# A three-stage kernel on one core: its last stage regrouped into steps of two or three score units

## The chip, the cores and the metric

The kernel runs on one core of a Trainium2 chip. A core has five engines that run side by side, each through its own list of instructions in order: TensorE (PE: matmuls and transposes; PEld is its weight load), VectorE (DVE), ScalarE (ACT), GpSimd (POOL) and SyncE (SP, which here issues nearly all DMAs). They wait for one another through semaphores. Matmul results land in PSUM, eight banks of 128 x 512 fp32; the rest lies in SBUF. The metric is the time of one execution on the device in microseconds (us).

## The reference, cut to what matters

Three layers for 8 batch entries of 576 tokens: a pooled attention, a gated MLP with a spatial mix (together the first stage of the kernel), and, in the second stage, a mixture of four attention experts:

```python
logits = x @ w_gate                       # (576, 4); the two best experts, softmax over them -> w
for e in range(4):
    q, k, v = x @ wq[e], x @ wk[e], x @ wv[e]           # (576, 64) each
    scores = scale * (q @ k.T); scores[causal] = -1e9
    a = exp(scores - max); a /= a.sum(-1) + 1e-09
    out += (1 if e chosen else 0) * w_e * (a @ v @ wo[e])
```

fp32 accuracy is kept by splitting operands into a high and a low part (names that end in h and l): most products are two or three matmuls.

## The kernel before, in words

The first stage (class PhaseA) ends at about 595 us and is not touched. The second stage (class PhaseB) takes one batch entry b after the other, and in each two pairs of experts, p = 0 and 1: sixteen half batches. The work of a half batch is

- `proj` (tile pj): q and k of the pair, each in two halves of 288 tokens, 12 matmuls a half; `put_q` and `put_k` split the result on ACT and DVE and send copies of it by DMA (kd, qz) that the scores read;
- nine score units u = 0 to 8 (table `QT`): a block of 128 tokens of one expert. u = 0 is the last 64 tokens of both experts (576 columns, two banks, tile s4 in the code), u = 1 to 4 are blocks of 512, 384, 256 and 128 columns of the first expert, u = 5 to 8 the same of the second;
- each unit is `score` (PE; then a DVE reduction on L831, or L822 and L824 for u = 0, that adds the mask and gives the minimum of the negated scores; then exp on ACT, L834, which also gives the row sum), `scale` (DVE adds 1e-9, L845 or L843, and takes the reciprocal, L846; POOL, or DVE where the sets `SDF` and `SDL` say so, multiplies the row by reciprocal and gate weight, L850), and `trans` (PE transposes of 128 x 128, L863 and L876; ACT copies the high part, DVE subtracts the low part: tiles pbh, pbl);
- `av` (tile av, L896): attention times values for one expert, in two column parts, from pbh and pbl; then tiles ah and al (L906, L907);
- once both pairs are done, `outp` (tile op, L918 to L920): four output columns f, each in two column parts of 6 matmuls, copied by ACT (L921) and sent out.

Values and gate of the next entry (`vproj`, tile vp, five token tiles; `gate`, a chain of small DVE instructions that ends in tiles gw and wl) are computed in the second half batch of the one before. Everything in PSUM takes the next of eight banks in turn (`bank`), so a PE instruction waits until the bank that was given out eight earlier has been read.

The order is written by hand in `run`, one unit per step: score of unit k, `scale` of unit k - 1, then the fillers that the tables `FILL`, `FIRSTF` (first entry) and `LASTF` (last entry) name for this place (10 to 13: the four proj halves of pair 1; 00 to 03: those of the next entry's pair 0; v0 to v4 and g: values and gate; o: outp; x: loads), then av where it is due, and the transposes of unit k - 3 (`LAG`). `PRE` is what runs ahead of the first score. Within that order each engine's own list is merged by the scheduling layer.

Of the kernel before, what the change touches and what calls it, by code (L numbers as in the profile page):

```python
# [8 lines left out]
F32 = mybir.dt.float32  # L9
# [589 lines left out]
LAG = 3  # L599
# [9 lines left out]
PRE = 'v0 00 01 02 03 v1 v2 v3 v4 g'  # L609
# [3 lines left out]
class PhaseB:  # L613


    def __init__(self, ctx, tc, w, ins, x2d, out, ident):
# [3 lines left out]
        self.X, self.QK, self.V, self.GW, self.U, self.PT, self.AV, self.AH = {}, {}, {}, {}, {}, {}, {}, {}  # L620
# [185 lines left out]
    def score(self, b, p, u):  # L806
# [4 lines left out]
        st = w.tile([128, 8], F32, name="sm", bufs=4)  # L811
        pt = self.pr[:, (18 * b + 9 * p + u) % 5]
        if e == 2:
            parts = []
            for s in (slice(0, 320), slice(320, S)):
# [6 lines left out]
            nc.vector.tensor_tensor_reduce(o, o, self.ml, -0.125, BIG, OP.add, OP.min, st[:, 4:5])  # L822
            o = parts[0][0]
            nc.vector.tensor_tensor_reduce(o, o, self.mk[:, 0:1].to_broadcast([128, 320]), -0.125, st[:, 4:5],  # L824
                                           OP.add, OP.min, st[:, 0:1])
        else:
# [4 lines left out]
            nc.vector.tensor_tensor_reduce(o, o, self.mk[:, 576 - n:576], -0.125, BIG, OP.add, OP.min, st[:, 0:1])  # L831
            parts = [(o, slice(0, n))]
        for j, (o, s) in enumerate(parts):
            nc.scalar.activation(pt[:, s], o, AF.Exp, bias=st[:, 0:1], scale=-1.0, accum_out=st[:, 1 + 4 * j:2 + 4 * j])  # L834
        self.U[b, p, u] = (pt, st)

    def scale(self, b, p, u):
        nc = self.nc
        i, e = QT[u]
        pt, st = self.U[b, p, u]  # L840
        gw, wl = self.GW[b]
        if e == 2:
            nc.vector.tensor_scalar(st[:, 2:3], st[:, 1:2], 1e-9, st[:, 5:6], op0=OP.add, op1=OP.add)  # L843
        else:
            nc.vector.tensor_scalar(st[:, 2:3], st[:, 1:2], 1e-9, None, op0=OP.add)  # L845
        nc.vector.reciprocal(st[:, 3:4], st[:, 2:3])  # L846
# [3 lines left out]
         nc.gpsimd).tensor_scalar(pt[:, :n], pt[:, :n], st[:, 3:4], g, op0=OP.mult, op1=OP.mult)  # L850

    def trans(self, b, p, u):
        nc, w = self.nc, self.w
        i, e = QT[u]
        pt, _ = self.U.pop((b, p, u))
# [53 lines left out]
    def outp(self, b, f):  # L909
        nc, w = self.nc, self.w  # L910
        c = slice(128 * f, 128 * f + 128)
        o = w.tile([128, S], F32, tag="vg", name="o", bufs=3)
        for lo, up in AVS:
            ps = self.bank("op")[:, :up - lo]
            s = slice(lo, up)
            for p in range(2):
                ah, al = self.AH[b, p]
                nc.tensor.matmul(ps, self.wo[0][:, p, c], ah[:, s], start=p == 0, stop=False)  # L918
                nc.tensor.matmul(ps, self.wo[1][:, p, c], ah[:, s], start=False, stop=False)
                nc.tensor.matmul(ps, self.wo[0][:, p, c], al[:, s], start=False, stop=p == 1)  # L920
            nc.scalar.activation(o[:, s], ps, AF.Copy)  # L921
        nc.sync.dma_start(self.out[b, :, f], o)

    def run(self):
# [6 lines left out]
        units = [(b, p, u) for b in range(B) for p in range(2) for u in range(9)]  # L931
        def item(b, x):
# [4 lines left out]
            if x[0] == "1":  # L937
                return [part(b, 1)[int(x[1])]]
            if b + 1 == B:
                return []  # L940
# [5 lines left out]
        for x in PRE.split():  # L946
            for f in item(0 if x[0] == "1" else -1, x):
                f()
        for k in range(len(units) + LAG + 1):
            if k < len(units):  # L950
# [55 lines left out]
```

## Time and profile before

| | us |
|---|---|
| median of 3 runs (lowest, highest) | 986.61 (985.52, 988.78) |
| the profiled execution: its time | 986.47 |
| its span | 984.4 |
| the second stage in it, from its first matmul to the end | about 388 |

| engine | PE | PEld | DVE | ACT | POOL |
|---|---|---|---|---|---|
| busy us of the span | 915.4 | 863.3 | 715.2 | 511.1 | 490.4 |

The shares are averages over stages. In the second stage PE, DVE and ACT are all far busier than POOL. Matmuls overlap in the pipeline: how long one takes of PE's time is read from start to start of neighbours, not from its duration; the same holds, to a smaller degree, for DVE and ACT.

### The profile page before, as it was taken

Reading aid. Unit: us, or ns where it says so; the run is one execution under the profiler, and the core shown is the slowest. Engines: PE = TensorE matmul, PEld = TensorE weight load, DVE = VectorE, ACT = ScalarE, POOL = GpSimd, SP = SyncE. Lnnn points to the kernel's source line nnn. Section 1 sums busy time; section 2 is a strip of 40 time slices with the busy share of each in tenths; the row PEclk is TensorE's granted clock in tenths of the full one; section 3 lists DMA queues with packets and bytes.
Section 4 is the critical chain, followed back from the end, with each engine's and each line's share of the span. In section 5 each row is a group of like instructions: output and inputs, shape, how many; then the busy total and the mean of one; then the engine's idle time right before and its main releaser. Section 6 shows DMA issues by size and latency. Waiting matters only on the chain.

```text
span 984.4 us, 18357 instructions
## 1 busy us (share of the span) xinstructions
PE 915.4 (93%) x6488; PEld 863.3 (88%) x6488; DVE 715.2 (73%) x1901; ACT 511.1 (52%) x1291; POOL 490.4 (50%) x670
## 2 busy tenths in 40 slices
PE   4577899999999999999999999799999999999997
PEld 3366889989989999899899899799999999899987
DVE  6998747757567567476577524998979797979785
ACT  5576334334243343242342433576767676767776
POOL 6863727648369367375584450234434242525221
PEclk9589899999999999999999999999999999999999
DMA  9430321302302304122024012324233323322121
GB/s 331 186 101 22 101 88 47 128 26 81 110 20 71 118 12 141 45 82 99 31 62 121 1 52 70 84 48 118 72 112 72 116 74 96 84 84 84 48 60 73
DMA packets 37819, 82.92 MB, mean 84 GB/s; under 512 B 4960, under 2 KB 11104, under 8 KB 36832
## 3 DMA queue, kind: packets, MB, share of 16 engines
q1 hardware_dynamic: 37584, 81.75, 26.5%
q8 instruction: 52, 0.85, 0.4%
q14 instruction: 39, 0.32, 0.1%
q10 hardware_dynamic: 144, 0.00, 0.0%
HBM read 49.23 MB, written 18.87 MB: 69 GB/s over the span
## 4 chain that ended last, share of the span: by engine, by line
PE 57%; DVE 25%; ACT 8%; POOL 5%; issue 4%; DMA 1%; SPq 0%; POOLq 0%; ACTq 0%; DVEq 0%
PE op L445 4%; PE op L446 3%; PE op L447 3%; PE sp L420 3%; PE sp L422 3%; PE sp L421 3%; PE sc L230 3%; PE av L896 3%; DVE vnl L390 2%; DVE vnh L392 2%; ACT pr L834 2%; PE t L876 2%; PE tr L281 2%; DVE bs L376 2%; PE pj L705 2%
## 5 line engine op out<-in xcount | busy, mean ns | idle before, releaser
L850 POOL TENSOR_SCALAR pr<-pr,sm,gw 128x128 f32<-128x128 f32 (+3 forms) x119 | 77.9, 655 | 157.6 <-DVE sm L846 127.1
L834 ACT ACTIVATE pr<-s,sm 128x256 f32<-128x256 f32 (+4 forms) x160 | 83.0, 520 | 42.0 <-DVE sm L845 17.1
L332 POOL TENSOR_TENSOR xu<-x 128x576 f32<-128x576 f32 x28 | 39.2, 1428 | 98.3 <-DVE x L327 85.4
L446 PE MATMUL op<-g,woh 128*128 128x288 f32 x256 | 76.6, 301 | 4.2 <-POOL g L433 3.8
L420 PE MATMUL sp<-wsh,vnh 128*128 128x288 f32 x256 | 78.4, 306 | 1.6 <-ACT vnh L388 1.6
L404 PE MATMUL up<-x,wih 128*128 128x288 f32 x256 | 76.9, 301 | 2.4 <-ACT vg L364 2.2
L445 PE MATMUL op<-g,woh 128*128 128x288 f32 x256 | 78.2, 308 | 0.0
L421 PE MATMUL sp<-wsh,vnl 128*128 128x288 f32 x256 | 76.1, 297 | 0.0
L422 PE MATMUL sp<-wsl,vnh 128*128 128x288 f32 x256 | 75.9, 297 | 0.0
L406 PE MATMUL up<-x,wil 128*128 128x288 f32 x256 | 75.7, 296 | 0.0
L705 PE MATMUL pj<-xbh,wql 128*128 128x288 f32 x256 | 75.5, 295 | 0.0
L704 PE MATMUL pj<-xbl,wqh 128*128 128x288 f32 x256 | 75.5, 295 | 0.0
L703 PE MATMUL pj<-xbh,wqh 128*128 128x288 f32 x256 | 75.5, 295 | 0.0
L405 PE MATMUL up<-x,wih 128*128 128x288 f32 x256 | 75.1, 293 | 0.0
L447 PE MATMUL op<-g,wol 128*128 128x288 f32 x256 | 75.0, 297 | 0.0
L282 ACT ACTIVATE pth<-tr 128x640 fp32r<-128x640 f32 (+1 forms) x40 | 26.2, 654 | 79.6 <-PE tr L281 70.0
L876 PE MATMUL t<-ident,pr 128*128 128x128 f32 x320 | 57.9, 280 | 9.4 <-POOL pr L850 6.0
L831 DVE CUSTOM_DVE_ANT_0 s<-s,mk 128x512 f32<-128x512 f32 (+3 forms) x128 | 62.5, 488 | 0.4
L881 DVE TENSOR_TENSOR pbl<-t,pbh 128x512 fp32r<-128x512 f32 (+3 forms) x128 | 60.7, 484 | 2.4 <-ACT pbh L880 1.4
L230 PE MATMUL sc<-kbd,qt 128*128 128x144 f32 (+1 forms) x320 | 50.3, 303 | 10.9 <-DMA qt<-q_in 8.5
L361 PE MATMUL vp<-wih,x 128*128 128x512 f32 x128 | 52.0, 406 | 6.2 <-ACT wih L128 5.0
L896 PE MATMUL av<-pbh,vt 128*128 128x320 f32 (+4 forms) x224 | 55.6, 278 | 2.4 <-ACT pbh L880 2.4
(247 smaller groups left out, 3380.3 us busy)
## 6 DMA issues: line engine op xcount, KB each, us to landing
kraw<-k_in SPq DMA_DIRECT2D x16, 576.0 KB, 3.8
x<-x SPq DMA_DIRECT2D x32, 288.0 KB, 2.1
xb<-x SPq DMA_DIRECT2D x32, 288.0 KB, 3.0
kd<-scr SPq DMA_DIRECT2D x64, 144.0 KB, 2.5
out<-o SPq DMA_DIRECT2D x32, 288.0 KB, 2.2
vraw<-v_in SPq DMA_DIRECT2D x16, 512.0 KB, 4.1
qt<-q_in SPq DMA_DIRECT2D x7, 1152.0 KB, 6.9
st<-w_in_in SPq DMA_DIRECT2D x8, 512.0 KB, 8.9
```

The costliest lines, as they stand in the source:

```text
L230: nc.tensor.matmul(ps[:m, p // 2, (p % 2) * 144:(p % 2) * 144 + 144], qt[:, p, o:o + m], kbd[:, p, :], start=p % 2 == 0, stop=True, skip_g ...
L420: nc.tensor.matmul(o, vh[:, k, c], self.ws[0][:, k, s], start=k == 0, stop=False)
L421: nc.tensor.matmul(o, vl[:, k, c], self.ws[0][:, k, s], start=False, stop=False)
L422: nc.tensor.matmul(o, vh[:, k, c], self.ws[1][:, k, s], start=False, stop=False)
L445: nc.tensor.matmul(o, self.wo[0][:, k, c], gh[:, s], start=k == 0, stop=False)
L446: nc.tensor.matmul(o, self.wo[0][:, k, c], gl[:, s], start=False, stop=False)
L447: nc.tensor.matmul(o, self.wo[1][:, k, c], gh[:, s], start=False, stop=k == 3)
L705: nc.tensor.matmul(ps, self.wq[1][:, kc, c], xh[:, s], start=False, stop=kc == 3)
L834: nc.scalar.activation(pt[:, s], o, AF.Exp, bias=st[:, 0:1], scale=-1.0, accum_out=st[:, 1 + 4 * j:2 + 4 * j])
L850: nc.gpsimd).tensor_scalar(pt[:, :n], pt[:, :n], st[:, 3:4], g, op0=OP.mult, op1=OP.mult)
L876: nc.tensor.transpose(ps[:, j], pt[:, 128 * j:128 * j + 128], self.ident)
L896: nc.tensor.matmul(ps[:, s - lo:], vt[:, j, 2 * p + e].rearrange("p a d -> p (a d)"), t[:, e, j * PTS + s:j * PTS + up], start=j == 0 and ...
```

## The change: groups of units, other fillers, halves of two output columns

- A step is now a group of units: (0, 1), (2, 3), (4, 5), (6, 7, 8). It issues all scores of the group, then one addition and one reciprocal for the whole group (the new `sums`, on a shared tile sm), then the products with the gate weight, then the fillers, then the transposes of the group before.
- `av` is a filler ("a") in the first two steps of the following half batch; all four `outp` of the entry before stand in the last two steps of p = 0.
- In the first entry only two value tiles run ahead of the scores; the other three and the gate (V2 V3 V4 G) stand in the first step, and the products of that step behind them. Proj halves of k run ahead of those of q.
- At the end, output columns 0 and 1 are begun with pair 0 alone and finished after the last av, and the last entry's outputs go out by column parts.

```diff
-LAG = 3
...
-FILL = (('', '12 10 11', '', '13', 'x0', 'x1', 'o3 o1 x2 x3 o0', '', ''), ('v0', 'v1 00 02', '01 o2', '03', '', '', '', 'v2 v3', 'v4 g'))
-FIRSTF = (('10', '11', '12', '13', 'x0', '', 'x1 x2', 'x3', ''), ('v0 00', '', '01 02 v1', '03', '', '', '', 'v2 v3', 'v4 g'))
-LASTF = (('', '10 12 11', '', '', '13', '', 'o1', '', 'o0'), ('', '', '', '', '', 'o2', '', '', 'o3'))
+GROUPS = ((0, 1), (2, 3), (4, 5), (6, 7, 8))
+FILL = (('12 a', '13 a', '10 11 x0 o0', 'x1 o1 x2 o2 x3 o3'), ('v0 a v1', '02 a', '03 00 01', 'v2 v3 v4 g'))
+FIRSTF = (('V2 V3 V4 G', '12 13', '10 11 x0 x1', 'x2 x3'), ('v0 a v1', '02 a', '03 00 01', 'v2 v3 v4 g'))
+LASTF = (('12 a', '13 a', '10 11', 'o0'), ('a', 'o1 a', 'o2', ''))
...
-PRE = 'v0 00 01 02 03 v1 v2 v3 v4 g'
+PRE = '02 03 00 01 v0 v1'
...
-    def score(self, b, p, u):
+    def score(self, b, p, u, st, n_):
...
-        st = w.tile([128, 8], F32, name="sm", bufs=4)
+        mx = st[:, n_:n_ + 1]
...
+    def sums(self, units, st):
+        nc, n = self.nc, len(units)
+        if QT[units[0][2]][1] == 2:
+            nc.vector.tensor_scalar(st[:, 3:4], st[:, 3:4], st[:, 13:14], None, op0=OP.add)
+        nc.vector.tensor_scalar(st[:, 6:6 + n], st[:, 3:3 + n], 1e-9, None, op0=OP.add)
+        nc.vector.reciprocal(st[:, 9:9 + n], st[:, 6:6 + n])
...
+    def outp(self, b, f, pairs=(0, 1)):
...
+            if pairs[0] == 0:
+                self.OP[f, g] = self.bank("op")[:, :up - lo]
+            ps = self.OP[f, g]
+            for p in pairs:
...
+                if last:
+                    nc.sync.dma_start(self.out[b, :, f, s], o[:, s])
...
+        for b, p, g in steps:
+            new = [(b, p, u) for u in GROUPS[g]]
+            st = self.w.tile([128, 14], F32, name="sm", bufs=3)
+            for n_, u in enumerate(new):
+                self.score(*u, st, n_)
+            if b + p + g:
+                self.scales(new, st)
+            for x in (LASTF if b + 1 == B else FILL if b else FIRSTF)[p][g].split():
+                for f in item(b, p, g, x):
+                    f()
+            if not b + p + g:
+                self.scales(new, st)
+            for u in last:
+                self.trans(*u)
+            last = new
+        self.outp(B - 2, 3)
+        for s in range(2):
+            self.av(B - 1, 1, 0, s)
+        for u in last:
+            self.trans(*u)
+        for f in range(2):
+            self.outp(B - 1, f, (0,))
+        for s in range(2):
+            self.av(B - 1, 1, 1, s)
         for f in range(4):
-            self.outp(B - 1, f)
+            self.outp(B - 1, f, (0, 1) if f > 1 else (1,))
```

The first place is PE where the first output column of the entry before is begun (tiles: t transposes, s scores, op output). Before, it stands late in the first half batch, behind the scores of unit 6:

```order
L863 MATMUL t_6932<-ident,pr 64x128
L829 MATMUL s<-kd,qs_5907 128x128
L830 MATMUL s<-qs_5907,qzvhi_5915 128x128
L876 MATMUL t<-ident,pr 128x128 x4
L829 MATMUL s<-kd,qs_5907 128x512
L830 MATMUL s<-qs_5907,qzvlo_5916 128x512
L876 MATMUL t<-ident,pr 128x128 x3
L829 MATMUL s<-kd,qs_5907 128x384
L830 MATMUL s<-qs_5907,qzvlo_5916 128x384
L918 MATMUL op<-ah,wqh 128x256
```

Now the same column stands in the third step, behind two proj halves (24 matmuls of pj, of which the first three are shown):

```order
L885 MATMUL t<-ident,pr 128x128 x4
L830 MATMUL s<-kd,qs_5907 128x128
L831 MATMUL s<-qs_5907,qzvhi_5915 128x128
L830 MATMUL s<-kd,qs_5907 128x512
L831 MATMUL s<-qs_5907,qzvlo_5916 128x512
L703 MATMUL pj<-xbh,wqh 128x288
L704 MATMUL pj<-xbl,wqh 128x288
L705 MATMUL pj<-xbh,wql 128x288
...
L931 MATMUL op<-ah,wqh 128x256
```

Transposes and scores no longer alternate, and between the av that makes ah and the first op there are now nine transposes, two scores and two proj halves.

The second place is DVE in the middle of a half batch (sm holds minima, sums and reciprocals; pbl is the low part of the transposed rows). Before:

```order
L831 ISA s,sm<-s,mk 128x512
L831 ISA sm 128x1
L845 TENSOR_SCALAR sm<-sm 128x1
L881 TENSOR_TENSOR pbl<-t,pbh 128x3x128
L846 RECIPROCAL sm<-sm 128x1
L831 ISA s,sm<-s,mk 128x384
L831 ISA sm 128x1
L845 TENSOR_SCALAR sm<-sm 128x1
L881 TENSOR_TENSOR pbl<-t,pbh 128x2x128
L846 RECIPROCAL sm<-sm 128x1
```

Now, in the second step of a half batch:

```order
L832 ISA s,sm<-s,mk 128x384
L832 ISA sm 128x1
L832 ISA s,sm<-s,mk 128x256
L832 ISA sm 128x1
L843 TENSOR_SCALAR sm<-sm 128x2
L844 RECIPROCAL sm<-sm 128x2
L735 TENSOR_TENSOR qs_5907<-pj,scr 128x288
L910 TENSOR_TENSOR scr<-av,scr 64x256
```

The addition no longer belongs to a unit scored earlier: it stands directly behind the reductions of its own group, and needs the exps of that group, which need those reductions.

The third place is DVE in the first entry, behind the gate chain (gg, gs, gw, wl are its tiles; pr holds the rows of the units). Before, the two products of units 0 and 1 (L850) stand well behind it:

```order
L799 TENSOR_TENSOR gw<-gg,gs 128x20
L719 TENSOR_TENSOR qs_5911<-pj,qs_5911 64x288
L802 COPY wl<-gw 64x2 x2
L721 TENSOR_TENSOR qs_5911<-pj,qs_5911 64x288
L846 RECIPROCAL sm<-sm 128x1
L845 TENSOR_SCALAR sm<-sm 128x1
L719 TENSOR_TENSOR qs_5911<-pj,qs_5911 64x288
L850 TENSOR_SCALAR pr<-pr,sm,wl 128x576
```

Now (L859 is the product), with a proj eviction of the next half batch inside the chain:

```order
L735 TENSOR_TENSOR qs_5911<-pj,scr 128x288
L793 TENSOR_REDUCE gg<-ga 128x20
L794 SCALAR_TENSOR_TENSOR gg<-gg 128x20
L795 TENSOR_REDUCE gs<-gg 128x5
L796 TENSOR_SCALAR gs<-gs 128x5
L797 RECIPROCAL gs<-gs 128x5
L799 TENSOR_TENSOR gw<-gg,gs 128x20
L802 COPY wl<-gw 64x2 x2
L859 TENSOR_SCALAR pr<-pr,sm,gw 128x512
L859 TENSOR_SCALAR pr<-pr,sm,wl 128x576
```

The row of unit 0, which is transposed first, is now multiplied last.

## Rows read from the trace of the kernel before

**Rows 1.** Engines by window: first, a middle and the last entry; columns stand ahead.

```profile
core 0: us, PE busy (x) PEld busy (x) DVE busy (x) ACT busy (x) POOL busy (x), PEclk, DMA share, GB/s
609.30:651.70 42.40, 36.85 (x269) 34.86 (x267) 37.78 (x147) 28.29 (x88) 11.07 (x15) 0.96 0.27 69
...
698.50:745.30 46.80, 45.33 (x349) 43.95 (x347) 39.81 (x153) 33.63 (x107) 18.42 (x26) 1.00 0.32 88
...
932.60:984.40 51.80, 43.96 (x325) 41.55 (x323) 37.91 (x152) 37.16 (x113) 10.98 (x18) 1.00 0.20 64
```

**Rows 2.** Waits of PE, entries 1 to 6: total us, times, longest us.

```profile
PE op L918 <- DVE scr L901: 4.5, 6, 0.8
PE t L876 <- POOL pr L850: 3.4, 6, 0.6
```

**Rows 3.** Timeline of PE in entry 2: start, us, instruction, [idle before <-releaser].

```profile
709.44 0.30 PE L896 MATMUL av<-pbh,vt 128*128 128x320 f32 x1
709.87 0.39 PE L896 MATMUL av<-pbl,vt 128*128 128x256 f32 x1
...
713.21 0.34 PE L830 MATMUL s<-qs,qzvlo 128*128 128x384 f32 x1
714.30 0.39 PE L918 MATMUL op<-ah,wqh 128*128 128x256 f32 x1 [0.75 <-DVE scr L901]
714.52 0.28 PE L919 MATMUL op<-ah,wql 128*128 128x256 f32 x1
...
720.00 0.27 PE L830 MATMUL s<-qs,qzvlo 128*128 128x128 f32 x1
720.87 0.33 PE L876 MATMUL t<-ident,pr 128*128 128x128 f32 x1 [0.59 <-POOL pr L850]
```

**Rows 4.** DVE groups by shape, entries 1 to 6: busy us, mean ns | idle before.

```profile
L846 DVE RECIPROCAL sm<-sm 128x1 f32<-128x1 f32 x108 | 17.6, 163 | 2.1
L845 DVE TENSOR_SCALAR sm<-sm 128x1 f32<-128x1 f32 x96 | 14.3, 149 | 13.9 <-ACT pr L834 13.9
L831 DVE CUSTOM_DVE_ANT_0 s<-s,mk 128x256 f32<-128x256 f32 x24 | 10.2, 425 | 0.2
```

**Rows 5.** ACT groups by shape, entries 1 to 6.

```profile
L834 ACT ACTIVATION_READ_ACCUMULATOR pr<-s,sm 128x1 f32 x120 | 23.7, 198 | 0.0
L834 ACT ACTIVATE pr<-s,sm 128x256 f32<-128x256 f32 x36 | 17.1, 475 | 2.2 <-DVE sm L845 1.0
L834 ACT ACTIVATE pr<-s,sm 128x384 f32<-128x384 f32 x24 | 14.0, 584 | 6.8 <-DVE sm L831 6.7
```

**Rows 6.** Timeline of PE in the first entry.

```profile
627.23 1.09 PE L876 MATMUL t<-ident,pr 128*128 128x128 f32 x4 [2.59 <-DVE pr L850]
```

**Rows 7.** Windows behind that wait, columns as in the first group.

```profile
626.00:628.00 2.00, 0.77 (x5) 0.80 (x5) 2.00 (x4) 0.00 (x0) 1.26 (x2) 0.68 0.00 0
628.00:630.00 2.00, 2.00 (x11) 2.00 (x10) 2.00 (x10) 1.05 (x3) 0.60 (x1) 0.50 0.81 242
```

**Rows 8.** Timeline of DVE in the first entry: gate chain and products.

```profile
610.28 0.43 DVE L762 TENSOR_TENSOR vs<-vp,vs 128x260 f32<-128x260 f32 x1 [0.87 <-ACT vs L761]
...
615.61 0.34 DVE L802 COPY wl<-gw 64x2 f32<-64x2 f32 x2
...
618.91 0.54 DVE L850 TENSOR_SCALAR pr<-pr,sm,gw 128x512 f32<-128x512 f32 x1
...
625.46 1.62 DVE L850 TENSOR_SCALAR pr<-pr,sm,gw 128x512 f32<-128x512 f32 x1
```

**Rows 9.** Timeline of POOL beside the last of these.

```profile
625.20 1.60 POOL L633 TENSOR_TENSOR xbl<-xb,xbh 128x576 fp32r<-128x576 f32 x1 [1.12 <-DVE sm L846]
```

**Rows 10.** Timeline of PE in the last entry.

```profile
966.07 0.33 PE L876 MATMUL t<-ident,pr 128*128 128x128 f32 x1 [0.72 <-POOL pr L850]
971.78 0.54 PE L896 MATMUL av<-pbh,vt 128*128 128x256 f32 x2 [0.78 <-ACT pbh L880]
```

**Rows 11.** POOL groups by shape, entries 1 to 6.

```profile
L850 POOL TENSOR_SCALAR pr<-pr,sm,gw 128x512 f32<-128x512 f32 x25 | 23.0, 920 | 21.8 <-DVE sm L846 18.1 <-PE t L876 3.1 <-PE vp L773 0.5
```

More of the change, by code (lines that the diff above doesn't have):

```diff
@@ L854, in trans @@
         i, e = QT[u]
-        pt, _ = self.U.pop((b, p, u))
+        pt = self.U.pop((b, p, u))
         if u == 0:
@@ L907, in av @@
             (nc.vector if ALV else nc.gpsimd).tensor_sub(al[:, lo:up], a[:, lo:up], ah[:, lo:up].bitcast(F32))
-    def outp(self, b, f):
+    def outp(self, b, f, pairs=(0, 1)):
         nc, w = self.nc, self.w
         c = slice(128 * f, 128 * f + 128)
-        o = w.tile([128, S], F32, tag="vg", name="o", bufs=3)
-        for lo, up in AVS:
-            ps = self.bank("op")[:, :up - lo]
+        last = b + 1 == B
+        if pairs[-1] == 1:
+            o = w.tile([128, S], F32, tag="vg", name="o", bufs=3)
+        for g, (lo, up) in enumerate(AVS):
             s = slice(lo, up)
-            for p in range(2):
+            if pairs[0] == 0:
+                self.OP[f, g] = self.bank("op")[:, :up - lo]
+            ps = self.OP[f, g]
+            for p in pairs:
                 ah, al = self.AH[b, p]
[L918 to L922, printed above, removed]
+                nc.tensor.matmul(ps, self.wo[0][:, p, c], ah[:, s], start=p == 0, stop=False, skip_group_check=True)
+                nc.tensor.matmul(ps, self.wo[1][:, p, c], ah[:, s], start=False, stop=False, skip_group_check=True)
+                nc.tensor.matmul(ps, self.wo[0][:, p, c], al[:, s], start=False, stop=p == 1, skip_group_check=True)
+            if pairs[-1] == 1:
+                nc.scalar.activation(o[:, s], ps, AF.Copy)
+                if last:
+                    nc.sync.dma_start(self.out[b, :, f, s], o[:, s])
+        if pairs[-1] == 1 and not last:
+            nc.sync.dma_start(self.out[b, :, f], o)
     def run(self):
@@ L930, in run, with item @@
         vpart = lambda b: [lambda t=t: self.vproj(b, t) for t in range(NT)]
-        units = [(b, p, u) for b in range(B) for p in range(2) for u in range(9)]
-        def item(b, x):
+        steps = [(b, p, g) for b in range(B) for p in range(2) for g in range(4)]
+        def item(b, p, g, x):
+            if x == "a":
+                b, p = (b, 0) if p else (b - 1, 1)
+                return [lambda s=s: self.av(b, p, g, s) for s in range(2)]
             if x[0] == "x":
@@ L938, in item @@
                 return [part(b, 1)[int(x[1])]]
+            if x[0] == "V":
+                return [vpart(b)[int(x[1])]]
+            if x[0] == "G":
+                return [lambda: self.gate(b)]
             if b + 1 == B:
@@ L946, in run @@
         for x in PRE.split():
[L947 removed]
+            for f in item(-1, 0, 0, x):
                 f()
[L949 to L966 removed]
+        last = []
+        for b, p, g in steps:
[22 more added lines that the diff above has]
+            self.av(B - 1, 1, 1, s)
         for f in range(4):
[L968 removed]
+            self.outp(B - 1, f, (0, 1) if f > 1 else (1,))
 def host_b(inputs, a):
```

46 lines of the change are left out of this document (15 added, 31 removed).

## The prediction, as recorded before the run

> **What bounds the kernel now.** I read the engines by window first. In a middle entry PE is busy 45.33 of 46.80 us at a granted clock of 1.00, DVE 39.81, ACT 33.63, POOL 18.42 [rows 1]; so PE sets the pace, but DVE is not far behind, and a list that is worked in order can hold PE up long before it is full. The reader is to see three stretches: a first entry that keeps PE waiting 42.40 - 36.85 = 5.6 us, six middle entries with 1.5 us each, and a last one with 51.80 - 43.96 = 7.8 us (its output goes out behind its last matmul).
>
> Next I read what ended PE's waits in entries 1 to 6: six waits for the tiles of the pair just attended (op for DVE's scr, 4.5 us) and six of a transpose for its row's product on POOL (3.4 us) [rows 2]. The timeline of one entry shows their size from start to start, which idle time understates: 713.21 to 714.30 is 1.09 us, 720.00 to 720.87 is 0.87, and a third, at the av, 0.43 from 709.44 to 709.87 [rows 3]. Unhindered, neighbours stand 0.1 to 0.2 apart (714.30 to 714.52 is 0.22, still with the pipeline filling). So an entry loses 1.8 to 2.1 us; I take 2.0, and its work without waits is 46.8 - 2.0 = 44.8 us. No edit removes matmuls, so 6 x 2.0 = 12 us is all that the six middle entries can give.
>
> **The change part by part.** *Middle entries, waits removed.* The op no longer follows the av that feeds it: nine transposes, two scores and two proj halves stand between (24 matmuls at 45.33 / 349 = 0.13 us [rows 1] are 3.1), against a wait of 0.75 [rows 3]. That wait goes. A transpose now comes one whole step, some 5 us, after its group's scores are done; the product on POOL has until then, and POOL is busy 18.42 of 46.80 [rows 1]. That wait goes too. Price so far: 2.0 x 6 = 12 us of gain.
>
> *Middle entries, waits added.* DVE's addition stands directly behind the reductions of its own group and waits for that group's exps. Two units of 384 and 256 columns: the exps take 0.58 and 0.48, and reading their sums 0.20 each, part of it under the next instruction [rows 5], so about 1.2 us behind the first reduction; the second reduction covers 0.34 to 0.43 of it [rows 4]; DVE stands about 0.9 us, where nothing else was put between. A group of three or with the two-part unit 0 costs 1.0 to 1.5. Queued behind the addition are the evictions of proj, value and av tiles and the low parts of the transposes, and for these PE waits, either because av reads them or because a bank is still held. By the order, in four of an entry's eight steps other ready work (casts, q and k evictions, value tiles, parts of the gate) was merged in between, which leaves 0 to 0.5 each; the other four cost about 1.0, 1.0, 1.0 and 1.45. Sum 4.5 to 5.5 us of standing DVE per entry.
>
> On the other side DVE saves small instructions: per entry 16 single additions (96 / 6) and 18 reciprocals, 0.15 and 0.16 us each, become 8 of each, (16 - 8) x 0.15 + (18 - 8) x 0.16 = 2.8 us by durations [rows 4]; they overlap, so some 2 of it is real. Before, DVE already stood 13.9 / 6 = 2.3 us per entry for exps [rows 4]. DVE then needs 39.8 - 2 + 5 = 43 us, under PE's 44.8, but tight where the gate (a chain that belongs to the second half batch) meets the two dearest stops. I worked the DVE list through there by hand with these durations: at the second step of the next entry the three low parts that av needs come 0.7 us late; elsewhere the bank or tile is free in time, by 0.1 to 3 us. I add 0.2 for the near ones: 0.9 us of new waits per entry. Bounds: 0 (everything is hidden) and 3.2 (all eight steps cost what a bare one does, worked out under the rivals). Middle entries: 6 x (2.0 - 0.9) = 6.6 us of gain, between 12 and -7.
>
> *First entry.* Here the gate moved behind the first scores. From the sum of the last value tile on DVE (610.28) to the end of wl (615.95) the chain took 5.7 us, and a product 0.54 [rows 8]; DVE had waited 0.87 for the copy of the last value matmul, so that lies 0.8 ahead. In the new order PE has, from that matmul on, two scores and two proj halves, about 4 us, and then wants the row of unit 0, which DVE multiplies last. So PE waits 0.8 + 5.7 + 1.1 - 4 = 3.6 us there. Then, by the same working of the lists, a small wait for POOL's product of unit 4 behind a load's subtraction (0.6) and one for the q copy of the next pair (0.9): 5.1 in all. Before, PE stood 5.6 us [rows 1], longest 2.59 us for a product on DVE [rows 6].
>
> What a product costs beside POOL is in the trace: alone it took 0.54, and 1.62 at 625.46 [rows 8], in the time when POOL subtracted (625.20 to 626.80) [rows 9]. POOL's products of units 2 and 3 wait for the same gate weights and so start beside DVE's two. I take 0.7 of delay, between 0 and 1.1. [...]
>
> The 2.59 us wait also cost clock: it was granted 0.68 and then 0.50, the lower level, in the 4 us behind it [rows 7], (0.77 x 0.32 / 0.68) + 2.0 x 0.5 = about 1.4 us. A wait of 4.3 us should bring the same, so this cancels. First entry: 5.1 + 0.7 - 5.6 = 0.2 us dearer, 2 either way.
>
> *Last entry.* Removed: the transpose's wait for POOL and the av's wait behind the last transposes (0.72 and 0.78) [rows 10], the latter because six matmuls each of two columns now stand in front. Added: the last half batch has few fillers, so its transposes of units 4 and 5 follow their scores by only twelve op matmuls, five transposes and three scores, about 1.6 + 0.5 + 1.0 = 3 us, while the reductions, exps, addition and POOL's products (0.92 for 512 columns [rows 11]) of that group need about 5, an estimate from [rows 4, 5, 11]: 2.2 us; and an av at its start waits 1.2 for a low part that is queued behind exps, which ACT starts only after an output copy. I cost it at 0, 2.5 either way. The outputs by parts shorten only the last transfer: 0.1, left out.
>
> The sum: 986.47 - 6.6 + 0.2 + 0 = 980.1 us by the profiled execution, which lies 0.14 under the median of the runs. I predict 980.
>
> **The rivals.** *All hidden.* DVE's stops fall into time in which PE's results were not there anyway. For it: before, DVE had 46.80 - 39.81 = 7.0 idle us per entry [rows 1]. Against: four bare stops. Then the middle entries give 12, the ends 2: 972.
>
> *DVE becomes the bound (slower).* Place: the addition behind its group's reductions, in all middle entries. If the merged order helps nowhere, a half batch stops 1.45 + 1.0 + 1.0 + 1.0 us, an entry 8.9; and if of the other idle time (7.0 - 2.3 = 4.7 us) a quarter, 1.3, comes on top (an estimate), DVE needs 39.8 - 2 + 8.9 + 1.3 = 48 us: 1.2 more than before, 7 us in six entries, and 2 at the ends: 995; half-way, 990. It decides from about 9 us of standing DVE per entry on, against the 5 that I count. For it: late DVE work also delays ACT, and the last half batch already shows this in my own working.
>
> *The waits only change their name.* Each entry keeps about 2 us, now at av for low parts and at banks: 985 to 987. For it: DVE's busy time is so close to PE's.
>
> [...]
>
> **How the numbers follow.** The forecast (some of the waits gone) 0.50; all hidden 0.14; waits only renamed 0.20; DVE the bound 0.14; clock 0.02. A measurement here can tell about 0.3% (3 us) from nothing. The forecast's own range is 975 to 985: nearly nine tenths of it lie below 983.6. So faster 0.14 + 0.43 + 0.05 of the renamed = 0.62; slower is the clock's 0.02 and 0.12 of the DVE case = 0.14; same, the rest, 0.24. The range that should hold 8 in 10 goes to 970 below (all hidden, with ends a little better) and 990 above (half of the DVE case).
>
> **What would show it.** Right: in middle entries PE waits neither for scr at op nor for pr at a transpose, the period falls from 46.8 to about 45.7, DVE's idle time in front of the addition rises to 4 or 5 us an entry, and PE's largest remaining wait there is an av for pbl. In the first entry one wait of 3.6 to 4.5 us stands before the first transposes, with the clock low behind it. Wrong: a period of 46.8 or more with PE waiting for banks that DVE frees; a DVE that hardly stands at the additions; a granted clock under 1.00 in middle entries; or ends that move by more than 3 us.

## The result, and the profile after

| | before | after |
|---|---|---|
| median of 4 runs, us (lowest, highest) | 987.04 (985.52, 988.78) | 997.95 (995.96, 999.41) |
| the profiled execution: its time, its span | 986.47, 984.4 | 999.41, 997.6 |

The change makes the kernel slower: ratio 1.0114, 95% interval 1.0099 to 1.0129. The prediction (980, range 970 to 990) had it faster. The four runs before are the three of the first table and one more.

To see where, I cut each trace at the same four points: the last matmul of the first stage, the first score of entry 1, the first score of entry 7, and the end of the last matmul. Times are worked out from the starts of these instructions, in us.

| stretch | forecast of the change | before | after | difference |
|---|---|---|---|---|
| first stage (not touched) | 0 | 594.95 | 595.75 | +0.8 |
| to the first score of entry 1 | +0.2 | 56.73 | 58.92 | +2.2 |
| entries 1 to 6 | -6.6 | 280.97 | 287.36 | +6.4 |
| entry 7 to the last matmul | 0 | 47.76 | 51.61 | +3.9 |
| behind it | 0 | 4.0 | 4.0 | 0 |

The first stage is the same in every kernel of this document and took 593.2 to 596.9 us in the profiled executions, so from one profile to another the stretches compare better than the whole times.

The engines by window after, first, a middle and the last entry (columns as in [rows 1], to which they answer):

```profile
606.20:654.70 48.50, 42.67 (x301) 41.29 (x299) 38.05 (x133) 28.82 (x89) 10.74 (x14) 0.89 0.26 63
703.30:751.00 47.70, 45.42 (x348) 44.32 (x346) 38.81 (x135) 33.12 (x107) 17.10 (x25) 1.00 0.31 87
942.00:997.60 55.60, 46.19 (x325) 43.33 (x323) 37.63 (x131) 36.29 (x112) 11.97 (x18) 0.96 0.19 59
```

In a middle entry PE has the same to do (45.42 us against 45.33) and DVE less (38.81 against 39.81), and yet it takes 47.7 us instead of 46.80. So something is held up, and the view of PE's waits (entries 1 to 6) says where PE notices it:

```profile
PE s L830 <- DVE qs L721: 7.5, 6, 1.3
PE av L905 <- DVE pbl L890: 5.7, 6, 1.0
PE t L885 <- ACT pr L835: 0.4, 1, 0.4
```

Both old waits [rows 2] are gone, as forecast: no op waits for scr, no transpose for POOL's product. Two new ones stand there, six times each. The timeline of PE in entry 2 has their sizes from start to start:

```profile
710.80 0.39 PE L905 MATMUL av<-pbh,vt 128*128 128x256 f32 x1
712.13 0.39 PE L905 MATMUL av<-pbl,vt 128*128 128x256 f32 x1 [0.95 <-DVE pbl L890]
...
721.21 0.28 PE L831 MATMUL s<-qs,qzvlo 128*128 128x256 f32 x1
722.74 0.30 PE L830 MATMUL s<-kd,qs 128*128 128x128 f32 x1 [1.25 <-DVE qs L721]
```

The av (1.33 between starts, some 1.2 of it wait) is the one that I forecast with 0.7. The score (1.53, some 1.4 wait) was not in the forecast: its bank is held by a proj half until DVE's L721 has read it. What DVE did ahead of that:

```profile
720.28 0.45 DVE L719 TENSOR_TENSOR qs<-pj,qs 64x288 fp32r<-64x288 f32 x1
720.97 1.14 DVE L843 TENSOR_SCALAR sm<-sm 128x2 f32<-128x2 f32 x1 [0.24 <-ACT pr L835]
722.13 0.46 DVE L721 TENSOR_TENSOR qs<-pj,qs 64x288 fp32r<-64x288 f32 x1
```

The reader is to see the duration in the middle row. This is the addition of 1e-9 to two sums per partition; it waited 0.24 us for the exp, as a stop of that kind should, and then lasted 1.14 us, where the others take 0.17. It ends when a POOL instruction ends, a subtraction over 576 columns (two in this row, the first until 722.08):

```profile
720.66 2.78 POOL L633 TENSOR_TENSOR xbl<-xb,xbh 128x576 fp32r<-128x576 f32 x2
```

No wait is recorded for it, since it stands in the instruction's own duration; the view of waits names the next victim, L721. In every middle entry it is the same place. Over the whole second stage 8 of the 48 additions of two columns begin beside a running POOL instruction; each of the 8 ends 20 to 30 ns behind it (0.29 to 1.15 us), and none of the other 40 lasts over 0.172. The groups of DVE (entries 1 to 6; compare [rows 4]) show it as a mean of 331 ns with two columns against 166 with three, and the standing that I had forecast as 4.5 to 5.5 us an entry as (14.4 + 8.4 + 4.0) / 6 = 4.5:

```profile
L843 DVE TENSOR_SCALAR sm<-sm 128x2 f32<-128x2 f32 x36 | 11.9, 331 | 14.6 <-ACT pr L835 14.4
L842 DVE TENSOR_SCALAR sm<-sm 128x1 f32<-128x1 f32 x12 | 2.5, 209 | 8.4 <-ACT pr L835 8.4
L843 DVE TENSOR_SCALAR sm<-sm 128x3 f32<-128x3 f32 x13 | 2.2, 166 | 4.0 <-ACT pr L835 4.0
```

At the start, the wait behind the gate's chain came as worked out (4.20, forecast 3.6 + 0.7; before it was [rows 6]), and the clock granted behind it was 0.50 for six us, where [rows 7] showed a fall of about four. Behind the next two waits, 0.73 us for a product (628.70) and 0.90 at a score (630.47), it fell a second time, to 0.66 over five us. First the timeline of PE, then two windows of the kernel after:

```profile
619.45 0.87 PE L872 MATMUL t<-ident,pr 128*128 128x128 f32 x3 [4.20 <-DVE pr L859]
```

```profile
618.00:624.00 6.00, 4.55 (x19) 4.35 (x20) 3.88 (x9) 1.81 (x5) 0.99 (x2) 0.50 0.26 62
...
630.00:635.00 5.00, 4.53 (x22) 4.34 (x23) 5.00 (x17) 2.00 (x9) 1.57 (x3) 0.66 0.57 162
```

At the end, the transposes of units 4 and 5 wait 1.79 and 0.42 us (2.2 forecast), and the clock falls there too (0.72 over the six us from 978), which the forecast did not have; before, the last entry ran at 1.00 throughout [rows 1, 10]:

```profile
977.87 0.33 PE L885 MATMUL t<-ident,pr 128*128 128x128 f32 x1 [1.79 <-POOL pr L859]
978.61 0.73 PE L885 MATMUL t<-ident,pr 128*128 128x128 f32 x4 [0.42 <-POOL pr L859]
```

```profile
978.00:984.00 6.00, 5.58 (x32) 5.39 (x33) 3.46 (x11) 3.66 (x11) 1.38 (x2) 0.72 0.07 28
980.00:984.00 4.00, 4.00 (x24) 4.00 (x24) 2.43 (x6) 1.98 (x5) 0.71 (x1) 0.69 0.11 42
```

### The profile page after: what moved, and what is told of

It is laid out like the page before. It is cut to its first block, busy times and chain, and to the rows that moved or that the text cites. A ratio compares the mean times of both kernels' runs of the same rounds, so it can differ in the third digit from the quotient of the medians.

```text
span 997.6 us, 18226 instructions
## 1 busy us (share of the span) xinstructions
PE 923.2 (93%) x6488; PEld 872.1 (87%) x6488; DVE 707.8 (71%) x1757; ACT 507.4 (51%) x1291; POOL 483.7 (48%) x670
## 4 chain that ended last, share of the span: by engine, by line
PE 64%; DVE 21%; ACT 6%; POOL 4%; issue 3%; DMA 1%; SPq 0%; ACTq 0%; POOLq 0%; DVEq 0%
PE av L905 4%; PE op L445 4%; PE op L446 3%; PE op L447 3%; PE sp L422 3%; PE sp L420 3%; PE sp L421 3%; PE sc L230 3%; PE t L885 3%; PE pj L703 3%; PE pj L705 3%; PE pj L704 3%; DVE vnl L390 2%; DVE vnh L392 2%; DVE bs L376 2%
## 5 line engine op out<-in xcount | busy, mean ns | idle before, releaser
L859 POOL TENSOR_SCALAR pr<-pr,sm,gw 128x128 f32<-128x128 f32 (+3 forms) x119 | 73.4, 625 | 175.5 <-DVE sm L844 101.7
L890 DVE TENSOR_TENSOR pbl<-t,pbh 128x512 fp32r<-128x512 f32 (+3 forms) x128 | 58.2, 484 | 10.6 <-ACT pbh L889 9.2
L230 PEld LDWEIGHTS sc<-kbd,qt 128*128 128x128 f32 (+1 forms) x320 | 44.0, 191 | 15.3 <-issue 9.1
```

The costliest lines, as they stand in the source:

```text
L230: nc.tensor.matmul(ps[:m, p // 2, (p % 2) * 144:(p % 2) * 144 + 144], qt[:, p, o:o + m], kbd[:, p, :], start=p % 2 == 0, stop=True, skip_g ...
```

## The experiments

Theory: what the forecast lacks in the middle entries is the addition that POOL's subtraction stretches, to 1.13 to 1.15 us in each of them. Rivals: DVE is late by its amount of work, or by the exps alone; the start and the end carry the loss. All runs were timed against the kernel before on the same chip; its median was 986.6 to 987.2.

| run | median us | ratio to before (95%) | to entry 1 | entries 1 to 6 | entry 7 |
|---|---|---|---|---|---|
| after | 997.95 | 1.0114 (1.0099 to 1.0129) | 58.92 | 287.36 | 51.61 |
| e1_no_add | 988.14 | 1.0010 (1.0001 to 1.0018) | 56.26 | 280.99 | 49.47 |
| e2_gate | 999.92 | 1.0130 (1.0115 to 1.0144) | 59.03 | 289.19 | 50.44 |
| e3_first | 994.24 | 1.0076 (1.0063 to 1.0088) | 55.80 | 287.47 | 51.69 |
| e4_tail | 996.84 | 1.0099 (1.0086 to 1.0112) | 58.92 | 287.62 | 49.55 |
| c1_before_no_add | 983.94 | 0.9976 (0.9965 to 0.9988) | 54.92 | 280.61 | 47.76 |
| e6_sub_on_dve | 998.51 | 1.0129 (1.0112 to 1.0147) | 58.81 | 289.85 | 50.21 |
| e7_av_later | 1000.73 | 1.0128 (1.0110 to 1.0147) | 56.40 | 290.05 | 49.41 |
| e8_all | 1000.17 | 1.0133 (1.0118 to 1.0149) | 56.20 | 292.01 | 50.37 |
| e9_no_pool_sub | 998.74 | 1.0115 (1.0101 to 1.0128) | 58.87 | 289.36 | 50.38 |
| e10_best | 982.85 | 0.9948 (0.9935 to 0.9962) | 53.54 | 278.47 | 48.98 |
| c2_op_later | 985.49 | 0.9990 (0.9981 to 0.9999) | 54.94 | 282.30 | 47.77 |
| e11_idle_add | 994.92 | 1.0074 (1.0060 to 1.0087) | 58.12 | 286.68 | 49.34 |
| e12_single_adds | 992.64 | 1.0060 (1.0047 to 1.0074) | 58.95 | 281.43 | 51.34 |
| c3_before_wide | 989.91 | 1.0027 (1.0016 to 1.0037) | 57.27 | 283.70 | 48.17 |

The last three columns are the stretches of the first table, from each run's one profiled execution.

**The addition taken out (e1_no_add).**

```diff
-        nc.vector.tensor_scalar(st[:, 6:6 + n], st[:, 3:3 + n], 1e-9, None, op0=OP.add)
-        nc.vector.reciprocal(st[:, 9:9 + n], st[:, 6:6 + n])
+        nc.vector.reciprocal(st[:, 9:9 + n], st[:, 3:3 + n])
```

> The changed kernel without the addition of 1e-9 to the groups' sums: the reciprocal reads the sums directly (a sum is at least 1, so the addition changes no bit of it). Theory (the addition stands for POOL's subtraction, not only for the exps): in six middle entries the addition of the third step lasted 1.13 us instead of 0.17 while POOL ran a 576-wide subtraction; reciprocals seen beside such subtractions lasted 0.17. Without it the PE wait of 1.40 us before the third score of the fourth step falls to 0.4 to 0.5 in every entry, about 1 us less per entry, 6 to 7 us in all: 990 to 992. Rival (the list on DVE is late because of the exps alone): the wait stays near 1.4 and the time falls by the eight instructions of 0.1 us that are gone at most, under 1 us: 997.

It gave 9.8 us, more than expected. DVE, POOL and PE at the same place:

```profile
715.68 0.17 DVE L843 RECIPROCAL sm<-sm 128x2 f32<-128x2 f32 x1 [0.24 <-ACT pr L835]
```

```profile
715.38 1.41 POOL L633 TENSOR_TENSOR xbl<-xb,xbh 128x576 fp32r<-128x576 f32 x1
```

```profile
716.49 0.30 PE L830 MATMUL s<-kd,qs 128*128 128x128 f32 x1 [0.28 <-DVE qs L721]
```

The reciprocal, two columns wide as well, runs beside the same subtraction in 0.17 us, and the bank wait falls from 1.25 to 0.28. Entries 1 to 6 lose 6.4 us, as expected; start and end another 2.7 and 2.1, which the theory did not have; most of that is the clock (see the account of the first and the last entry below).

**The addition kept, its result unused (e11_idle_add).** To part the instruction from the link that it forms in the chain from exp to product.

```diff
-        nc.vector.reciprocal(st[:, 9:9 + n], st[:, 6:6 + n])
+        nc.vector.reciprocal(st[:, 9:9 + n], st[:, 3:3 + n])
```

> The changed kernel with its additions of 1e-9 in their old places on DVE, but with nobody reading their result: the reciprocal takes the sums directly, as in the run without the additions (988.1). It parts what that run removed: the instruction on DVE, and a link in the chain from exp to product. Theory (in middle entries the instruction costs, because it holds DVE while POOL's subtraction runs): they stay at 47.5 to 47.9 with the bank wait at 1.4; start and end, where the reciprocal could follow its addition only behind other work, gain 2 to 4: 994 to 996. Rival (the chain from the exp to the product is what was shortened): middle entries at 46.75, 988 to 989.

DVE, then PE:

```profile
720.42 1.13 DVE L843 TENSOR_SCALAR sm<-sm 128x2 f32<-128x2 f32 x1 [0.24 <-ACT pr L835]
721.46 0.15 DVE L844 RECIPROCAL sm<-sm 128x2 f32<-128x2 f32 x1
```

```profile
722.25 0.30 PE L830 MATMUL s<-kd,qs 128*128 128x128 f32 x1 [1.31 <-DVE qs L721]
```

Nobody reads the addition, and it still costs the middle entries 286.68 against 280.99: there it is the instruction, held on DVE, that costs, not the chain, as the theory had it (994.92). At the end the chain was what counted (49.34, as without the addition).

**Who holds it: POOL's subtractions on DVE (e6_sub_on_dve, e9_no_pool_sub).** `XV` says which of the four loads DVE subtracts; the first run has `(0, 1, 3)`, the second

```diff
-XV = (3,)
+XV = (0, 1, 2, 3)
```

My theory was that the addition lasts 0.17 us again where no subtraction of POOL runs beside it, and that the time falls although DVE has more to do: to 992 to 995 in the first run, to 990 to 995 in the second.

> The changed kernel with the 576-wide subtractions of two more of the four loads on DVE instead of POOL, in entries from the second load on; all additions stay. It gives DVE, which is late, 1.5 us more work per entry. [...] Rival (DVE is late by the amount of its work): the waits grow by 0.7 to 1.5 us per entry, time 1002 to 1007.

> The changed kernel with the 576-wide subtractions of all four loads on DVE, from the second load on, so that POOL runs none beside the additions (with two of three moved, the third still met the addition, which lasted 1.07 us). It gives DVE some 2.3 us more work per entry than the changed kernel. [...] Rival (the length has another cause, or DVE's amount of work decides): additions stay near 1.1, or they are short and the time is 998 or more all the same.

In the first the one subtraction that was left still met the addition (1.07 us), and the time was 998.51, between the theory's 995 and the rival's 1002, so it told little. In the second, over the middle entries:

```profile
L843 DVE TENSOR_SCALAR sm<-sm x40: 168/169/172, 707.3 to 941.9; 128x2 f32<-128x2 f32 x30, 128x3 f32<-128x3 f32 x10
```

```profile
768.54 0.30 PE L830 MATMUL s<-kd,qs 128*128 128x128 f32 x1 [0.28 <-DVE qs L721]
```

The row gives least, median and longest in ns: no addition over 172, and the bank wait is as short as without the addition. So POOL's subtraction was what stretched it. The time did not fall: three subtractions more on DVE opened other waits (a transpose for an exp, up to 0.6, and several smaller ones; the av unchanged, 1.2). The expected 990 to 995 was wrong; both theory and rival hold in part, since DVE's amount of work counts as well.

**Where the same addition was short (e12_single_adds, c3_before_wide).** In the kernel before, 52 of the 96 additions of entries 1 to 6 began while a POOL instruction ran (35 of them over 0.2 us behind its start), six of them beside the same 576-wide subtraction, as here (DVE, then POOL), and none lasted over 0.156 us:

```profile
710.07 0.15 DVE L845 TENSOR_SCALAR sm<-sm 128x1 f32<-128x1 f32 x1
```

```profile
709.15 1.43 POOL L633 TENSOR_TENSOR xbl<-xb,xbh 128x576 fp32r<-128x576 f32 x1 [1.05 <-PE pj L704]
```

They differ in width: one column there, two in the change. So narrow the one and widen the other. If the width decides (my theory), no addition of the first run lasts over 0.2 us, and its time is 988 to 991; in the second one per middle entry, beside the 576-wide subtraction, lasts 0.8 us or more, and its time is 991 to 999.

```diff
-        nc.vector.tensor_scalar(st[:, 6:6 + n], st[:, 3:3 + n], 1e-9, None, op0=OP.add)
+        for j in range(n):
+            nc.vector.tensor_scalar(st[:, 6 + j:7 + j], st[:, 3 + j:4 + j], 1e-9, None, op0=OP.add)
```

> The changed kernel with the addition of a group's sums issued as two or three additions of one column each, in the same place (two or three instructions of 0.15 us instead of one of 0.17). [...] Rival (what decides is the place, beside the 576-wide subtraction): an addition of about 1.1 us stays in every entry, middle entries at 47.75 or more, time 998.

```diff
-            nc.vector.tensor_scalar(st[:, 2:3], st[:, 1:2], 1e-9, None, op0=OP.add)
-        nc.vector.reciprocal(st[:, 3:4], st[:, 2:3])
+            nc.vector.tensor_scalar(st[:, 6:8], st[:, 0:2], 1e-9, None, op0=OP.add)
+        nc.vector.reciprocal(st[:, 3:4], st[:, 2:3] if e == 2 else st[:, 7:8])
```

> The kernel before with its single additions widened to two columns (minimum and sum together, the reciprocal reads the second); nothing else. [...] Rival (width is nothing): all additions stay at 0.15 to 0.17 us and the time at 986 to 988.

The additions of the two runs in the middle entries (narrowed, then widened):

```profile
L844 DVE TENSOR_SCALAR sm<-sm x92: 141/154/157, 705.9 to 940.1; 128x1 f32<-128x1 f32 x92
```

```profile
L845 DVE TENSOR_SCALAR sm<-sm x95: 148/169/583, 651.8 to 928.7; 128x2 f32<-128x2 f32 x95
```

The narrowed ones still met POOL: in the second stage 15 began beside a running POOL instruction, 12 of them beside a 576-wide subtraction, as here (DVE, then POOL), and none of the 15 lasted over 0.155 us:

```profile
718.16 0.15 DVE L844 TENSOR_SCALAR sm<-sm 128x1 f32<-128x1 f32 x1
```

```profile
717.96 1.41 POOL L633 TENSOR_TENSOR xbl<-xb,xbh 128x576 fp32r<-128x576 f32 x1
```

Both go the way of the theory: with one column the middle entries fall to 281.43 (start and end stay), with two those of the kernel before rise by 2.7 and the kernel by 2.9 us; there 29 of 128 additions last over 0.2 us, all beside a POOL instruction, and PE waits longer for scr at op than in [rows 2]:

```profile
PE op L918 <- DVE scr L901: 6.5, 6, 1.1
```

Both gain and loss are smaller than expected (992.64 against 988 to 991, 989.91 against 991 to 999): start and end had no part in the first, and in the second the additions met less of POOL's instructions (583 ns at most, where 0.8 us or more was expected).

**Control (c1_before_no_add).**

```diff
-            nc.vector.tensor_scalar(st[:, 2:3], st[:, 1:2], 1e-9, None, op0=OP.add)
-        nc.vector.reciprocal(st[:, 3:4], st[:, 2:3])
+            pass
+        nc.vector.reciprocal(st[:, 3:4], st[:, 2:3] if e == 2 else st[:, 1:2])
```

> Control: the kernel before without its additions of 1e-9 (16 single ones per entry; unit 0 keeps the addition of its two parts). Theory (what the addition costs is that it meets POOL's 576-wide subtractions on DVE, and in the kernel before none of the additions does: no addition there lasted over 0.16 us): the 96 additions of 0.15 us lie beside PE's work and the time stays within 1.5 us of 987. Rival (an addition behind the exps costs wherever it stands, since it lengthens the chain to each product): the six waits for the product of POOL shorten and the time falls by 3 us or more, as far as 980.

2.8 us faster, between the two: 1.8 at the start, 0.4 in six middle entries. At the start the longest wait for a product falls from 2.59 to 1.02 us, and the clock stays at 1.00 from 596 to 980 us; the fall that it saves, [rows 7], was priced in the forecast at about 1.4 us. The expectation was also wrong to say that no addition there meets a 576-wide subtraction; six do, and none lasts over 0.156 us.

**Start and end (e3_first, e4_tail).** For the start, all value tiles and the gate again ahead of the scores (and the first step's products again ahead of its fillers):

```diff
-FIRSTF = (('V2 V3 V4 G', '12 13', '10 11 x0 x1', 'x2 x3'), ...
-PRE = '02 03 00 01 v0 v1'
+FIRSTF = (('10', '12 13', '11 x0 x1', 'x2 x3'), ...
+PRE = 'v0 00 01 02 03 v1 v2 v3 v4 g'
```

> The changed kernel with the old order of its start: all value tiles, the four proj halves and the gate before the first scores; proj halves of the other pair behind them. Theory (the start loses about 3 us: a wait of 4.20 us for the DVE product behind the gate's chain, and a granted clock of 0.50 for about 6 us behind it): the stretch from 596 us to the first score of the second entry, 58.6 us now and 55.6 before the change, falls to 55 to 56.5, the time to 995. Rival (the old order loses as much by waiting for the first product and the group sums): 58 or more, time 998.

For the end, one output column a step earlier:

```diff
-LASTF = (..., ('a', 'o1 a', 'o2', ''))
+LASTF = (..., ('a', 'o1 a', 'o2 o3', ''))
...
-        self.outp(B - 2, 3)
```

> The changed kernel with the twelve matmuls of the one output column that stood behind the last scores' transposes moved in front of them, so that the products of units 4 and 5 of the last half batch have 24 matmuls (3.2 us) more or less to themselves. Theory (1.96 and 0.64 us of waiting for POOL's products there, and a granted clock of 0.69 in the 4 us behind it): both waits fall to under 1 us together, the clock stays at 1.00, and of the gain (1.6 + 1.3) the av that now follows the transposes at once gives back about 1 us: 996. Rival (the last entry is bound by the chain of DVE and ACT, and the wait only moves to the av): 998.

The start goes from 58.92 to 55.80, less than before the change, although a wait of 3.14 us for a product on POOL stands in the middle of it (624.97) and the clock falls behind it (0.50 from 626 to 630 us); the end from 51.61 to 49.55, with the clock at 1.00. Both theories hold in size; by the medians the gains are 3.7 and 1.1 us, the second smaller than the 2 that were expected.

**The av's wait (e2_gate, e7_av_later, e8_all).** Two ways to take it away: the gate earlier (first line of `+`), and, without the addition, one proj half ahead of the av (second).

```diff
-FILL = (('12 a', '13 a', '10 11 x0 o0', ...), ('v0 a v1', '02 a', '03 00 01', 'v2 v3 v4 g'))
+FILL = (('12 a', '13 a', '10 11 x0 o0', ...), ('v0 a v1', '02 a v2', '03 00 01 v3', 'v4 g'))
+FILL = (('12 a', '13 10 a', '11 x0 o0', ...), ('v0 a v1', '02 a', '03 00 01', 'v2 v3 v4 g'))
```

> The changed kernel with the value tiles of the next entry spread (one in the second and one in the third step of the second half batch), so that the gate's chain on DVE starts about 3 us earlier. Theory (the av of the second step waits 1.21 us for the low parts because the gate's chain stands in front of them on DVE): that wait falls to 0 to 0.4, the period of a middle entry from 47.75 to about 46.8, 992. Rival (the low parts are late because of the reductions of three groups and the two-part unit, whatever the gate does): the wait stays at about 1.2, the time at 997 to 999.

> The changed kernel without the addition of 1e-9, and with one proj half of the first half batch moved from the third step to the second, in front of the av that waits 1.25 us for the low parts. Theory (that wait is a lateness of DVE and ACT behind the gate's chain, caught up with within 1.6 us): it goes to 0 to 0.2, and the third step, shorter by the proj half, does not stall by more than 0.3 elsewhere: period of a middle entry 45.6 to 45.9 against 46.75 without the move, time 988 - 6 to 7 = 981 to 982. Rival (DVE is late through the whole half batch): the wait moves to the score's bank or to the transposes of the third step, period 46.5 or more, time 986 to 988.

The av's wait fell to 0.44 in the first, and a transpose's wait for exps (0.97) took its place: the chain now stood in front of the reductions. The time, 999.92, is above what theory and rival had. In the second the wait was gone, and the third step stalled instead, on DVE and then on PE:

```profile
762.32 1.18 DVE L915 TENSOR_TENSOR al<-scr,ah 128x320 fp32r<-128x320 f32 x1
```

```profile
763.56 0.41 PE L932 MATMUL op<-al,wqh 128*128 128x320 f32 x1 [0.35 <-DVE al L915]
...
766.83 0.33 PE L830 MATMUL s<-kd,qs 128*128 128x128 f32 x1 [0.97 <-ACT pr L835]
```

Here it is another DVE instruction, with both inputs in SBUF, that meets POOL's subtraction: 1.18 us where it takes 0.49. The rival of the second was right that the wait moves; but a middle entry took 48.0 us against 46.75 without the move, and the time, 1000.73, is far above its 986 to 988 (the profiled execution was the fastest of five, 996.20). e8_all added a new start and end to the second:

> The kernel of the run before (no addition, one proj half moved) with the old order of the start (gate before the first scores, one proj half of the other pair per step) and in the last entry the output columns moved in front of the products they wait beside. By the theories so far: 981.5 less 3 to 4 at the start and 1 to 3 at the end: 975 to 978, faster than both kernels. If start and end keep their waits under other names: 980 to 983.

It took 1000.17: the middle entries stall at L915 as before (1.19 us), and in three of them the clock fell too (0.66 from 818 to 823 us, for instance), which made them up to 1.6 us longer. Its start, with one proj half in each step, gained 0.2 over the run before, not 3 to 4.

**One part alone in the kernel before (c2_op_later).** Without the single additions, and

```diff
-FILL = (('', '12 10 11', '', '13', 'x0', 'x1', 'o3 o1 x2 x3 o0', '', ''), ...
+FILL = (('', '12 10 11', '', '13', 'x0', 'x1', 'x2 x3', 'o3 o1', 'o0'), ...
```

> The kernel before without its additions of 1e-9 (983.9) and with one part of the change alone: the output columns of the previous entry one or two score steps further from the av that feeds them; units stay single. Theory (the forecast's: the op's wait for DVE's tiles, 0.65 us per entry, is removed by distance): no wait for scr at op, 0.5 to 0.65 us per entry less, 980 to 981. Rival (DVE is late as such, and the wait turns up at the next consumer, a transpose or a bank): 983 to 985.

PE's waits in its middle entries:

```profile
PE av L896 <- DVE pbl L881: 2.8, 5, 0.6
PE t L876 <- POOL xbh L634: 2.4, 4, 0.6
PE s L829 <- ACT pr L834: 1.7, 5, 0.3
PE op L918 <- DVE pbh L872: 0.8, 5, 0.2
```

The wait for scr is gone, others have come (a transpose that waits for POOL's work on xbh, 0.6), and the entry is 0.3 us longer than in c1_before_no_add; the time, 985.49, is just above the rival's range. So the rival.

**A better one (e10_best).** No addition, the old start, the last entry's outputs a step earlier, and

```diff
-            nc.vector.tensor_copy(wl[64 * h:64 * h + 64], gw[:64, 4, h::2])
+            nc.scalar.activation(wl[64 * h:64 * h + 64], gw[:64, 4, h::2], AF.Copy)
```

> The changed kernel without the addition of 1e-9, with the old order of the start, the last entry's output columns one step earlier, and the two copies of the last tile's gate weights on ACT instead of DVE. Theory (the 1.25 us at the av of the second step come from DVE's list behind the gate's chain, 0.74 us of it these copies, which also meet POOL's product): that wait falls to 0.4 to 0.7, a middle entry to 46.0 to 46.3; 988 less 3 to 4 at the start, 1 to 2 at the end and 3 to 4 in the middle: 979 to 982. Rival (ACT, which writes the high parts of the same tiles before DVE takes the low ones, becomes later by the same amount): middle entries stay at 46.75, time 983 to 985.

982.85, faster than both kernels and between theory and rival; a middle entry takes 46.35 us, against 46.75 in e1_no_add. The av's wait is halved and is now shared by ACT and DVE:

```profile
750.58 0.38 PE L904 MATMUL av<-pbh,vt 128*128 128x256 f32 x1 [0.27 <-ACT pbh L888]
751.07 0.38 PE L904 MATMUL av<-pbl,vt 128*128 128x256 f32 x1
```

Against e1_no_add the start gained 2.7 us and the middle 2.5 (3 to 4 expected of each), the end 0.5 (1 to 2 expected); the end still loses 1.2 to the kernel before. Against c1_before_no_add (983.94, timed on another occasion) the lead is about 1 us, too little to tell.

## Why the prediction was wrong

*Waits removed, 2.0 an entry: right.* Both are gone. The work without waits, 44.8: right; 47.75 less 1.2, 1.4 and some 0.2 at an op is about 45.

*Waits added, "0.9 us of new waits per entry": wrong, this is the step that failed.* They are about 2.9, which is 47.75 - 44.8. Of the difference, 1.0 is the held addition, (287.36 - 281.43) / 6 as narrowing it shows. I had priced additions by the row of one column [rows 4] and taken the saving of eight of them as gain. The standing behind the exps (4 to 5 us) was right, and that DVE stays under PE too; the cost was not in how much DVE does but in what one instruction turned into. The other 1.0 is waits that I had put too small: the av's 1.2 instead of 0.7, of which the copies of wl took part (the second of the two, begun 0.24 us into POOL's product, lasts 0.57), and 0.6 at the bank and the op behind it, which stays without the addition. Six times 2.0, and 0.9 that only entry 1 takes more than the others (48.61 against 47.75), make the 13.0 us between the -6.6 of the forecast and the +6.4 measured. Two of the prediction's own signs of being wrong came: a period over 46.8 with PE waiting for a bank that DVE frees, and an end that moved by more than 3 us.

What a DVE instruction costs beside POOL I did weigh in the forecast, but only for the products at the start. The traces show more DVE instructions with two durations, the longest ones all beside a POOL instruction: 0.17 and up to 1.15 us for the addition of two columns, 0.16 and up to 0.58 for a copy of wl, 0.45 and up to 1.49 for a cast over 576 columns in the kernel before, 0.49 and 0.83 for a subtraction there (L907), 1.18 for the same one in e7_av_later (L915). That one column is not held the two runs on width show, whatever the reason (beside POOL none over 0.156 us with one column, up to 0.583 with two); of the 16 additions over three columns in the changed kernel none began beside a POOL instruction. With the 1.0 us an entry that the addition cost here the forecast would have been 986 (an estimate).

*The rivals.* With additions of one column the middle entries (281.43) are level with those of before (280.97): the rival that the waits only change their name was right for the order as such, and my 0.50 on the forecast too much. DVE as the bound named the right engine and sign, not the mechanism (in its working a quarter of 4.7 is 1.2, not 1.3; nothing hangs on it). The 0.02 that I gave the clock rested on no measurement: no run shows that nine transposes in a row lower it, and in the changed kernel it was 1.00 in all six middle entries.

*First entry, +0.2: 2.0 too small, just within the 2 that it had.* The standing of PE was right, 48.50 - 42.67 = 5.8 us by the window against 5.1 + 0.7, with waits of 4.20, 0.73 and 0.90 (the last for a low part, not for a q copy). That "this cancels" with the clock was wrong: 0.50 was granted for six us, where the fall before had lasted some four, and a second fall came. By the two windows shown that cost about 4.55 x 0.5 + 5.00 x (1 - 0.66) = 4.0 us (an estimate), against the 1.4 of before: enough for the whole loss.

*Last entry, 0: outside its bounds (+3.9).* Its two waits came, 1.79 + 0.42 us (forecast 2.2) and 0.55 at an av (1.2). Not in the forecast were, in its first half batch, an op that waits 0.89 for an exp to free a bank and a transpose that waits 0.58 for a q copy, and the clock behind the longest wait, about 6.00 x (1 - 0.72) = 1.7 us by the window shown (an estimate). Two us of the 3.9 come from the addition as a link: without it, or with its result unused, the stretch falls to 49.4. The clock then stays at 1.00 in it, so most of the two is the clock.

What stays open: e1_no_add and e11_idle_add, with the same edit of the chain, differ at the start by 1.9 us. In neither does the clock fall a second time. Behind the first wait it was granted 0.74, 0.50 and 0.91 in the three stretches of 2 us from 618 in e1_no_add, and 0.72, 0.50, 0.50 and 0.57 in the four of e11_idle_add, where PE stood through the first. That is about 1.7 and 2.8 us (an estimate, as above), so 1.1 of the 1.9 is clock. Why a wait of 3.94 us was followed by so much less of the low clock than one of 4.21, and where the other 0.8 lies, no run here shows.

## What to carry to other kernels

When instructions of one engine are merged, the merged form has to be measured and priced anew, beside what the other engines run at that moment: here an addition of two numbers per partition lasted 1.13 us where one of one number lasted 0.15, and it ended 20 to 30 ns behind POOL's subtraction. A wait that was moved came back at the next consumer in three runs here (e2_gate, e7_av_later, c2_op_later); first ask which engine's list is late, and take instructions off that list in front of the reader. And the 1.13 us of that addition stand in no idle time: look for the same form with two very different durations. Last, price a moved wait with the clock behind it: at the start of this kernel (0.50 and 0.66 granted) that was the whole loss.

## What the hardware showed that I had not expected

A DVE addition over two fp32 values per partition lasted 1.13 us when it began 0.3 us into a 1.4 us POOL subtraction, and one over one value 0.15 (e12_single_adds, 0.2 us into one of 1.41); a reciprocal of the same two columns lasted 0.17 (e1_no_add, 0.3 us into one of 1.41), and L721, which reads PSUM, 0.46 in each of the 14 places where it began beside POOL. Taking out an addition that changes no bit (the sums are at least 1) made the old kernel 2.8 us faster (c1_before_no_add), about half of it, by the estimate above, because the clock no longer fell at the start.
